# Casting loads in long runs, sliced attention, one-pass rsqrt and a moved g_norm in a linear-attention and bilinear-FFN kernel

## The chip, the cores and the metric

The kernel runs on one core of one Trainium2 chip. The metric is device time in microseconds (us), lower is better. Where several runs of a kernel exist, the median is given with the lowest and highest. Here a run counts as slow when it is over 1.5% above the fastest of the same kernel. One run of the kernel before (455.86 us, in the third group of rounds below) was slow; it is counted in the median of that group and left out of the ratios. The engines are called PE (TensorE), PEld (TensorE's weight loads), DVE (VectorE), ACT (ScalarE), POOL (GpSimd) and SP (SyncE), as the profile calls them.

## The reference, cut to what matters

```python
# q, k, v: (8 batches, 8 heads, 576, 64) fp32; g_norm: (64,)
kv  = np.einsum('bhsd,bhse->bhde', k, v)
out = np.einsum('bhsd,bhde->bhse', q, kv)
rms = np.sqrt(np.mean(out * out, axis=-1, keepdims=True) + 1e-06)
x   = (out / rms * g_norm)            # then (b, s, h*d): 4608 tokens x 512
a, b = x @ w_a, x @ w_b               # 512 x 1536 each
y   = (a * b) @ w_out                 # 1536 x 512, fp32 out
```

Linear attention per batch gives x. Two up projections are multiplied, and a down projection follows. In both kernels the matmuls run in bf16.

## The kernel before

q, k and v are loaded as fp32 by SyncE's queue, three loads per pair of heads and tensor. The two heads alternate in the tile, so that each run in it is one row of 64 values, 256 B. The matmuls read the upper halves of the fp32 words as bf16 (`bfview`). The weights go through GpSimd's queue, which casts them to bf16.

```python
def load_one(b, p, name, src):
    t = qkv_pool.tile([128, NCH + 1, 2, D], FP32, name=name, tag=name)
    for hl in range(2):
        nc.sync.dma_start(out=t[:, 0:NCH, hl, :],
            in_=src[b, 2 * p + hl, 0:SA, :].rearrange("(sp quar) d -> sp quar d", quar=NCH))
    nc.sync.dma_start(out=t[0:SB, NCH, :, :], ...)
```

Attention of a batch is a generator with three parts. The FFN units are another, and six units run after each part. A unit is one of 12 pairs of a/b products, or one of 4 output blocks, of a strip of 512 tokens. The last part of attention normalizes x. It takes 1/rms as Exp(-0.5 Ln(.)), four times per batch:

```python
for p in range(4):
    lns = asb_pool.tile([128, S], FP32, name="lns", tag="lns")
    nc.scalar.activation(lns[:, 0:SA], ssbA[p], AF.Ln, bias=eps_t, scale=1.0 / D)
    nc.scalar.activation(lns[:, SA:S], ssbB_sh[:, p, :], AF.Ln, bias=eps_t, scale=1.0 / D)
    sbc = asb_pool.tile([128, S], BF16, name="sbc", tag="sbc")
    nc.scalar.activation(sbc, lns, AF.Exp, scale=-0.5)
    nc.vector.tensor_mul(xt[p][:, tok0 : tok0 + S], xt[p][:, tok0 : tok0 + S], sbc)
yield
...
for b in range(B):                       # the schedule
    if b + 2 < B:
        loaded[b + 2] = load_b(b + 2)
    gen = attn_b(b, loaded.pop(b))
    for _ in gen:
        pump_ffn(6)
    ...                                  # strips whose tokens are done join the FFN queue
```

g_norm is multiplied into kv (a masked 128x128 VectorE multiply per pair of heads), and the ones matrix of the mean of squares is scaled by 1/g² to take it out again there.

Of the kernel before, what the change touches and what calls it, by code (L numbers as in the profile page):

```python
# [11 lines left out]


def bfview(t):
    u = t.bitcast(BF16)
    idx = tuple([slice(None)] * (len(u.shape) - 1) + [slice(1, None, 2)])
    return u[idx]
# [3 lines left out]
def kernel(  # L22
# [19 lines left out]
    SA = 512  # L42
    SB = S - SA
    NCH = S // 128
    STRIP = 512
    N_STRIP = n_tok // STRIP
    EPS = 1e-6

# [3 lines left out]
    qkv_pool = ctx.enter_context(tc.tile_pool(name="qkv", bufs=8))  # L52
    qst_pool = ctx.enter_context(tc.tile_pool(name="qst", bufs=12, space=bass.MemoryType.DRAM))
    asb_pool = ctx.enter_context(tc.tile_pool(name="asb", bufs=5))
    ab_pool = ctx.enter_context(tc.tile_pool(name="ab", bufs=2 * FC))
    osb_pool = ctx.enter_context(tc.tile_pool(name="osb", bufs=4))

    apsum = ctx.enter_context(tc.tile_pool(name="apsum", bufs=5, space=bass.MemoryType.PSUM))
    fpsum = ctx.enter_context(tc.tile_pool(name="fpsum", bufs=3, space=bass.MemoryType.PSUM))

    ident = const.tile([128, 128], BF16)
    make_identity(nc, ident)

    gmask = const.tile([128, 128], FP32)
    nc.vector.memset(gmask, 0.0)
    nc.gpsimd.dma_start(out=gmask[0:64, 0:64], in_=g_norm.partition_broadcast(64))
    nc.gpsimd.dma_start(out=gmask[64:128, 64:128], in_=g_norm.partition_broadcast(64))

    g_col = const.tile([128, 1], FP32)
    g_src = g_norm.rearrange("(d u) -> d u", u=1)  # L70
    nc.gpsimd.dma_start(out=g_col[0:64, :], in_=g_src)
    nc.gpsimd.dma_start(out=g_col[64:128, :], in_=g_src)
    invg2 = const.tile([128, 1], FP32)
    nc.vector.tensor_mul(invg2, g_col, g_col)
    nc.vector.reciprocal(invg2, invg2)
    bigmask = const.tile([128, 128], BF16)
    nc.vector.memset(bigmask, 0.0)
    nc.vector.memset(bigmask[0:64, 0:64], 1.0)
    nc.vector.memset(bigmask[64:128, 64:128], 1.0)
    nc.vector.tensor_scalar_mul(bigmask, in0=bigmask, scalar1=invg2)  # L80

    eps_t = const.tile([128, 1], FP32)
    nc.vector.memset(eps_t, EPS)

    wa_t = wpool.tile([128, KC, d_ff], BF16, name="wa_t")
    wb_t = wpool.tile([128, KC, d_ff], BF16, name="wb_t")
    wo_t = wpool.tile([128, FC, d_model], BF16, name="wo_t")

    def load_weights_ab():
        for kc in range(KC):  # L90
            nc.gpsimd.dma_start(
                out=wa_t[:, kc, :], in_=moe_w_a[kc * 128 : (kc + 1) * 128, :]
            )
            nc.gpsimd.dma_start(
                out=wb_t[:, kc, :], in_=moe_w_b[kc * 128 : (kc + 1) * 128, :]
            )

    def load_weights_o():
        for fc in range(FC):
            nc.gpsimd.dma_start(  # L100
                out=wo_t[:, fc, :], in_=moe_w_out[fc * 128 : (fc + 1) * 128, :]
            )

    xt = []
    for kc in range(KC):
        xt_t = xt_pool.tile([128, n_tok], BF16, name=f"xt{kc}", tag=f"xt{kc}")
        xt.append(xt_t)

    def load_one(b, p, name, src):
        t = qkv_pool.tile([128, NCH + 1, 2, D], FP32, name=name, tag=name)  # L110
        for hl in range(2):
            nc.sync.dma_start(  # L112
                out=t[:, 0:NCH, hl, :],
                in_=src[b, 2 * p + hl, 0:SA, :].rearrange(
                    "(sp quar) d -> sp quar d", quar=NCH
                ),
            )
        nc.sync.dma_start(  # L118
            out=t[0:SB, NCH, :, :],
            in_=src[b, 2 * p : 2 * p + 2, SA:S, :].rearrange("h sp d -> sp h d"),  # L120
        )
        return t

    def load_b(b):
        tiles = [{} for _ in range(4)]
        for p in range(4):
            tiles[p]["kt"] = load_one(b, p, "kt", k)
            tiles[p]["vt"] = load_one(b, p, "vt", v)
        for p in range(4):
            tiles[p]["qt"] = load_one(b, p, "qt", q)  # L130
        return tiles

    def attn_b(b, loaded):
        tok0 = b * S

        kv_sh = apsum.tile([128, 4, 128], FP32, name="kv_sh", tag="at")
        qT_ps = []
        for p in range(4):
            kt, vt = loaded[p]["kt"], loaded[p]["vt"]
            for c in range(NCH):  # L140
                nc.tensor.matmul(  # L141
                    kv_sh[:, p, :],
                    lhsT=bfview(kt[:, c, :, :]),
                    rhs=bfview(vt[:, c, :, :]),
                    start=(c == 0),
                    stop=False,
                )
            nc.tensor.matmul(  # L148
                kv_sh[:, p, :],
                lhsT=bfview(kt[0:SB, NCH, :, :]),  # L150
                rhs=bfview(vt[0:SB, NCH, :, :]),
                start=False,
                stop=True,
            )
        for p in range(4):
            qt = loaded[p]["qt"]
            qT = apsum.tile([128, S], BF16, name="qT_ps", tag="at")
            for c in range(NCH):
                nc.tensor.transpose(  # L159
                    qT[:, c * 128 : (c + 1) * 128], bfview(qt[:, c, :, :]), ident  # L160
                )
            nc.tensor.transpose(  # L162
                qT[:, SA:S], bfview(qt[0:SB, NCH, :, :]), ident[0:SB, 0:SB]
            )
            qT_ps.append(qT)
        kvg = []
        qT_sb = []
        for p in range(4):
            kvg_p = asb_pool.tile([128, 128], BF16, name="kvg", tag="kvg")
            nc.vector.tensor_mul(kvg_p, kv_sh[:, p, :], gmask)  # L170
            kvg.append(kvg_p)
            qs = asb_pool.tile([128, S], BF16, name="qT_sb", tag="qT_sb")
            nc.scalar.copy(qs, qT_ps[p])  # L173
            qT_sb.append(qs)
        yield

        xuA = []
        xuB_sh = apsum.tile([128, 4, SB], FP32, name="xuB_sh", tag="at")
        for p in range(4):
            xa = apsum.tile([128, SA], FP32, name="xuA", tag="at")  # L180
            nc.tensor.matmul(xa, lhsT=kvg[p], rhs=qT_sb[p][:, 0:SA], start=True, stop=True)  # L181
            nc.tensor.matmul(  # L182
                xuB_sh[:, p, :], lhsT=kvg[p], rhs=qT_sb[p][:, SA:S], start=True, stop=True
            )
            xuA.append(xa)
        sq_sb = []
        sqB_sh = asb_pool.tile([128, 4, SB], BF16, name="sqB_sh", tag="sqB_sh")
        nc.scalar.activation(sqB_sh, xuB_sh, AF.Square)
        for p in range(4):
            sq = asb_pool.tile([128, SA], BF16, name="sq_sb", tag="sq_sb")  # L190
            nc.scalar.activation(sq, xuA[p], AF.Square)  # L191
            sq_sb.append(sq)
            nc.vector.tensor_copy(xt[p][:, tok0 : tok0 + SA], xuA[p])
            nc.vector.tensor_copy(xt[p][:, tok0 + SA : tok0 + S], xuB_sh[:, p, :])
        yield

        ssbA = []
        ssbB_sh = apsum.tile([128, 4, SB], FP32, name="ssbB_sh", tag="at")
        nc.tensor.matmul(
            ssbB_sh.rearrange("a b c -> a (b c)"),  # L200
            lhsT=bigmask,
            rhs=sqB_sh.rearrange("a b c -> a (b c)"),
            start=True,
            stop=True,
        )
        for p in range(4):
            sa = apsum.tile([128, SA], FP32, name="ssbA", tag="at")
            nc.tensor.matmul(sa, lhsT=bigmask, rhs=sq_sb[p], start=True, stop=True)
            ssbA.append(sa)
        for p in range(4):  # L210
            lns = asb_pool.tile([128, S], FP32, name="lns", tag="lns")
            nc.scalar.activation(lns[:, 0:SA], ssbA[p], AF.Ln, bias=eps_t, scale=1.0 / D)  # L212
            nc.scalar.activation(  # L213
                lns[:, SA:S], ssbB_sh[:, p, :], AF.Ln, bias=eps_t, scale=1.0 / D
            )
            sbc = asb_pool.tile([128, S], BF16, name="sbc", tag="sbc")
            nc.scalar.activation(sbc, lns, AF.Exp, scale=-0.5)  # L217
            nc.vector.tensor_mul(  # L218
                xt[p][:, tok0 : tok0 + S], xt[p][:, tok0 : tok0 + S], sbc
            )  # L220
        yield

    def ffn_strip(s):
        t0 = s * STRIP
        ab_tiles = []
        for fc in range(FC):
# [68 lines left out]
    def pump_ffn(n):  # L295
        nonlocal cur_ffn
        for _ in range(n):
            while True:
                if cur_ffn is None:
                    if not ffn_q:  # L300
                        return
# [51 lines left out]
```

## Time and profile before

| | before |
|---|---|
| time, median of 3 runs | 450.46 us (450.39 to 453.36) |
| span of the profiled run | 446.9 us |
| PE busy | 349.9 us, 78% |
| ACT busy | 232.6 us, 52%, of which 65 table loads of 1.283 us: 83 us |
| steady TensorE work begins | about 70 us |

The page of the kernel before. The first line is each engine's busy time. The rows are 40 equal slices of the span (tenths for PE and PEclk, the granted TensorE clock). Then come the queues (packets, MB, share of 16 engines), the chain of waits by engine, and two groups (count, busy us, mean ns, idle before).

```profile
PE 349.9 (78%) x1720; PEld 160.6 (36%) x1720; DVE 142.6 (32%) x280; ACT 232.6 (52%) x341; POOL 13.6 (3%) x30
...
PE   0002548997699869987998699879986994999995
...
PEclk9999999999599979999999799989999999999999
...
GB/s 132 208 199 151 154 145 145 145 19 49 152 137 150 97 137 150 135 121 167 138 150 103 155 151 60 12 84 0 2 23 70 1 0 29 67 0 80 16 1 94
...
q1 hardware_dynamic: 115200, 28.33, 28.6%
...
PE 47%; ACT 31%; SPq 10%; issue 3%; DMA 3%; DVE 3%; ACTq 2%; DVEq 0%
...
L217 ACT ACT_TABLE_LOAD x32 | 41.1, 1283 | 0.6
L213 ACT ACT_TABLE_LOAD x30 | 38.5, 1283 | 0.5
```

Two losses stand in it. The PE row is empty for three slices and at most half full for the next three. After that it dips about once per batch, and the clock dips with it. ScalarE carries 31% of the chain.

The timeline of the kernel before, in three stretches (start us, duration us, engine, line, operation, output<-input, count, and in brackets the idle time before it and its releaser). SPq is SyncE's issuing; L213 and L217 are Ln and Exp:

```profile
45.07 1.28 SPq L112 DMA_DIRECT2D qt<-in_q_dram  x2
...
141.64 1.28 ACT L213 ACT_TABLE_LOAD   x1
142.94 0.31 ACT L213 ACTIVATE lns<-ssbB_sh,eps_t 128x64 f32<-128x64 f32 x1
143.15 1.26 ACT L212 ACTIVATE lns<-ssbA,eps_t 128x512 f32<-128x512 f32 x2
144.43 1.28 ACT L217 ACT_TABLE_LOAD   x1
145.72 0.68 ACT L217 ACTIVATE sbc<-lns 128x576 bf16<-128x576 f32 x1
...
159.57 0.59 PE L233 MATMUL a_ps<-xt_109,wa_t 128*128 128x512 bf16 x1 [1.34 <-DVE o_sb L263]
159.95 0.63 PE L233 MATMUL a_ps<-xt_110,wa_t 128*128 128x512 bf16 x1
...
162.87 0.38 PE L233 MATMUL a_ps<-xt_109,wa_t 128*128 128x512 bf16 x1
...
166.46 0.59 PE L241 MATMUL b_ps<-xt_109,wb_t 128*128 128x512 bf16 x1 [2.56 <-ACT a_sb L249]
```

SyncE issues a load every 0.63 us, and that alone sets the pace from 35 us on: the GB/s row is flat near 150 to about 90 us. From 141.6 to 158.4 us ScalarE does nothing but Ln, Exp and the loads between them, beside issuing two stores, and each pair of passes pays two loads.

The windows view of the kernel before shows what that costs TensorE. The first column is the stretch and the next its length, then busy us of PE, PEld, DVE, ACT and POOL with counts, then the granted clock, the DMA share and GB/s:

```profile
0.00:70.30 70.30, 16.39 (x72) 7.44 (x73) 6.97 (x24) 22.74 (x30) 13.59 (x30) 1.00 0.82 164
70.30:446.90 376.60, 333.54 (x1648) 153.19 (x1647) 135.62 (x256) 209.87 (x311) 0.00 (x0) 0.96 0.35 83
...
166.00:170.00 4.00, 3.54 (x10) 1.31 (x10) 1.38 (x2) 0.97 (x3) 0.00 (x0) 0.57 0.73 165
141.00:158.00 17.00, 15.86 (x97) 7.92 (x94) 2.67 (x5) 16.72 (x21) 0.00 (x0) 1.00 0.48 108
158.00:166.00 8.00, 4.56 (x15) 1.74 (x14) 3.05 (x8) 2.77 (x6) 0.00 (x0) 0.79 0.61 145
```

While ScalarE switches tables (141 to 158 us) TensorE still has queued units and is busy 15.9 of 17 us. The loss comes after it. From 158 to 170 us it is busy 8.1 of 12 us, and at a granted clock of 0.79 and then 0.57. The chain of waits there runs through what had piled up behind the passes on ScalarE: the issuing of stores, the landing of one (2.31 us) and four copies of q (2.25 us). After TensorE's wait at 159.57 us the matmuls run about 0.43 us apart up to 162.87 us, and then 0.216 us apart; after the wait at 166.46 us the same happens again. The Trainium skill, "TensorE: Matmul & The Clock Gate", Part 1, calls this a clock gate: the array starts at half rate and reaches the full one after about 3.4 us of sustained work. The trace agrees on that length (3.3 us).

### The profile page before, as it was taken

The page shows a single profiled execution, that of the slowest core. Times are in us where ns is not written, and L with a number is a line of the kernel's source. Part 1 is how long each engine was busy: PE and PEld are TensorE (multiplying, and loading weights), DVE is VectorE, ACT ScalarE, POOL GpSimd, SP SyncE. Part 2 cuts the span into 40 slices and gives each one's busy share as a digit, 9 for nine tenths or more (in the row PEclk, how much of TensorE's full clock was granted, in tenths as well). Part 3 has the DMA queues.
Part 4 walks back from the last instruction along what each step waited for, and adds up shares of the span by engine and source line. Part 5 has one row for each costly group of instructions (what it writes and reads, how often), then busy time and mean ns, then how long its engine had stood idle before and what let it go on. Part 6 is the DMA issues. An engine that isn't in the chain of part 4 may idle for free.

```text
span 446.9 us, 4884 instructions
## 1 busy us (share of the span) xinstructions
PE 349.9 (78%) x1720; PEld 160.6 (36%) x1720; DVE 142.6 (32%) x280; ACT 232.6 (52%) x341; POOL 13.6 (3%) x30
## 2 busy tenths in 40 slices
PE   0002548997699869987998699879986994999995
PEld 0001213443244424443444244434443441444442
DVE  0000212351353134414621353146214623332431
ACT  1000694589255944595579346945793587330320
POOL 6220000000000000000000000000000000000000
PEclk9999999999599979999999799989999999999999
DMA  6996666601566456556664662030002001202004
GB/s 132 208 199 151 154 145 145 145 19 49 152 137 150 97 137 150 135 121 167 138 150 103 155 151 60 12 84 0 2 23 70 1 0 29 67 0 80 16 1 94
DMA packets 123736, 42.83 MB, mean 96 GB/s; under 512 B 116512, under 2 KB 118080, under 8 KB 123712
## 3 DMA queue, kind: packets, MB, share of 16 engines
q1 hardware_dynamic: 115200, 28.33, 28.6%
q10 hardware_dynamic: 5504, 9.44, 7.9%
q0 software_dynamic: 3008, 4.75, 5.8%
q8 instruction: 13, 0.21, 0.2%
q14 instruction: 11, 0.09, 0.1%
HBM read 37.78 MB, written 9.44 MB: 106 GB/s over the span
## 4 chain that ended last, share of the span: by engine, by line
PE 47%; ACT 31%; SPq 10%; issue 3%; DMA 3%; DVE 3%; ACTq 2%; DVEq 0%
PE b_ps L241 20%; PE a_ps L233 20%; ACT L213 9%; ACT L217 8%; SPq L112 6%; ACT sbc L217 5%; PE o_ps L255 5%; SPq L118 4%; ACT lns L212 3%; ACT qT_sb L173 3%; ACTq L275 2%; ACT lns L213 2%; DVE o_sb L263 2%; PE xuA L181 2%; DMA out_dram<-o_sb 2%
## 5 line engine op out<-in xcount | busy, mean ns | idle before, releaser
L249 ACT CAST a_sb<-a_ps 128x512 bf16<-128x512 f32 x108 | 63.3, 593 | 113.7 <-PE a_ps L233 96.8
L241 PEld LDWEIGHTS <-wb_t 128*128 128x128 bf16 x432 | 43.7, 101 | 77.5 <-issue 31.8
L233 PEld LDWEIGHTS <-wa_t 128*128 128x128 bf16 x432 | 42.8, 101 | 66.0 <-issue 22.8
L173 ACT COPY qT_sb<-qT_ps 128x576 bf16<-128x576 bf16 x32 | 19.0, 647 | 77.6 <-PE qT_ps L162 53.3
L233 PE MATMUL a_ps<-xt_109,wa_t 128*128 128x512 bf16 x108 | 43.5, 403 | 14.9 <-DVE o_sb L263 14.0
L241 PE MATMUL b_ps<-xt_109,wb_t 128*128 128x512 bf16 x108 | 43.1, 400 | 13.0 <-ACT a_sb L249 12.9
L233 PE MATMUL a_ps<-xt_110,wa_t 128*128 128x512 bf16 x108 | 43.4, 402 | 3.1 <-DVE xt_110 L218 3.1
L233 PE MATMUL a_ps<-xt_111,wa_t 128*128 128x512 bf16 x108 | 43.2, 400 | 2.3 <-DVE xt_111 L218 2.3
L233 PE MATMUL a_ps<-xt_112,wa_t 128*128 128x512 bf16 x108 | 42.8, 397 | 1.9 <-DVE xt_112 L218 1.9
L141 PE MATMUL kv_sh<-vt,kt 128*128 128x128 bf16 x128 | 14.0, 236 | 37.5 <-DMA vt<-in_v_dram 37.5
L241 PE MATMUL b_ps<-xt_110,wb_t 128*128 128x512 bf16 x108 | 43.2, 400 | 0.0
L241 PE MATMUL b_ps<-xt_111,wb_t 128*128 128x512 bf16 x108 | 43.1, 399 | 0.0
L241 PE MATMUL b_ps<-xt_112,wb_t 128*128 128x512 bf16 x108 | 42.8, 397 | 0.0
L217 ACT ACT_TABLE_LOAD x32 | 41.1, 1283 | 0.6
L213 ACT ACT_TABLE_LOAD x30 | 38.5, 1283 | 0.5
L263 DVE COPY o_sb<-o_ps 128x512 f32<-128x512 f32 x36 | 23.5, 685 | 15.0 <-PE o_ps L255 15.0
L141 PEld LDWEIGHTS <-kt 128*128 128x128 bf16 x128 | 9.1, 104 | 42.8 <-issue 39.7
L217 ACT ACTIVATE sbc<-lns 128x576 bf16<-128x576 f32 x32 | 21.9, 683 | 0.4
L212 ACT ACTIVATE lns<-ssbA,eps_t 128x512 f32<-128x512 f32 x32 | 20.9, 682 | 0.0
L191 ACT ACTIVATE sq_sb<-xuA 128x512 bf16<-128x512 f32 x32 | 17.8, 610 | 5.0 <-PE xuB_sh L182 3.0
L159 PE MATMUL qT_ps<-ident,qt 128*128 128x128 bf16 x128 | 13.9, 237 | 5.0 <-DMA qt<-in_q_dram 5.0
L170 DVE TENSOR_TENSOR kvg<-kv_sh,gmask 128x128 bf16<-128x128 f32 x32 | 7.0, 281 | 33.6 <-PE kv_sh L148 33.6
(374 smaller groups left out, 423.9 us busy)
## 6 DMA issues: line engine op xcount, KB each, us to landing
kt<-in_k_dram SPq DMA_DIRECT2D x64, 128.0 KB, 2.9
vt<-in_v_dram SPq DMA_DIRECT2D x64, 128.0 KB, 2.8
qt<-in_q_dram SPq DMA_DIRECT2D x64, 128.0 KB, 2.8
out_dram<-o_sb ACTq DMA_DIRECT2D x40, 128.0 KB, 2.4
out_dram<-o_sb ACTq DMA_DIRECT2D x16, 256.0 KB, 2.5
wa_t<-in_moe_w_a_dram POOLq DMA_DIRECT2D x4, 384.0 KB, 11.2
wb_t<-in_moe_w_b_dram POOLq DMA_DIRECT2D x4, 384.0 KB, 12.8
wo_t<-in_moe_w_out_dram POOLq DMA_DIRECT2D x12, 128.0 KB, 8.3
```

Of the source, the lines that this page charges most:

```text
L112: nc.sync.dma_start(out=t[:, 0:NCH, hl, :], in_=src[b, 2 * p + hl, 0:SA, :].rearrange("(sp quar) d -> sp quar d", quar=NCH),)
L118: nc.sync.dma_start(out=t[0:SB, NCH, :, :], in_=src[b, 2 * p : 2 * p + 2, SA:S, :].rearrange("h sp d -> sp h d"),)
L141: nc.tensor.matmul(kv_sh[:, p, :], lhsT=bfview(kt[:, c, :, :]), rhs=bfview(vt[:, c, :, :]), start=(c == 0), stop=False,)
L173: nc.scalar.copy(qs, qT_ps[p])
L212: nc.scalar.activation(lns[:, 0:SA], ssbA[p], AF.Ln, bias=eps_t, scale=1.0 / D)
L213: nc.scalar.activation(lns[:, SA:S], ssbB_sh[:, p, :], AF.Ln, bias=eps_t, scale=1.0 / D)
L217: nc.scalar.activation(sbc, lns, AF.Exp, scale=-0.5)
L233: nc.tensor.matmul(a_ps, lhsT=wa_t[:, kc, fc * 128 : (fc + 1) * 128], rhs=xt[kc][:, t0 : t0 + STRIP], start=(kc == 0), stop=(kc == KC - 1),)
L241: nc.tensor.matmul(b_ps, lhsT=wb_t[:, kc, fc * 128 : (fc + 1) * 128], rhs=xt[kc][:, t0 : t0 + STRIP], start=(kc == 0), stop=(kc == KC - 1),)
L249: nc.scalar.copy(a_sb, a_ps)
L255: nc.tensor.matmul(o_ps, lhsT=ab_tiles[fc][:, g * 128 : (g + 1) * 128], rhs=wo_t[:, fc, :], start=(fc == 0), stop=(fc == FC - 1),)
L263: nc.vector.tensor_copy(o_sb, o_ps)
```

## The change

It has four intents, in one rewrite. (A slice is a piece of a batch's attention; "hoisted" below means that the build put an operation into an engine's queue ahead of work that does not need it.)

1. q, k and v come through GpSimd's casting queue, a half or a whole tensor of a batch per load, in runs of 1 KB read and 512 B written. VectorE then reorders k and q with copies.
2. Attention is cut into slices (kv of a pair, transposes of a pair, x of 288 columns), and one slice stands after every FFN unit.
3. Ln and Exp become one `Abs_reciprocal_sqrt`.
4. g_norm is applied at x, in the VectorE operation that also multiplies by 1/rms.

The rewrite also moves some work between engines: q's transposed copy goes to VectorE, kv's copy and half of the output copies to ScalarE, the stores to SyncE's queue. Weight loads get other shapes, and the buffers for TensorE's results are split in another way.

The core of the diff. Names of pools, the store's helper and the FFN loops, whose arithmetic is the same, are cut:

```diff
-    def load_one(b, p, name, src):
-        t = qkv_pool.tile([128, NCH + 1, 2, D], FP32, name=name, tag=name)
-        for hl in range(2):
-            nc.sync.dma_start(out=t[:, 0:NCH, hl, :], ...)
+    def load_b(b, parts):
+        for name in ("k", "v", "q"):
+            tiles[name] = qkv_pool.tile([128, H, NCH + 1, D], BF16, name=name + "t", tag=name)
+            if name != "v":
+                tiles[name + "r"] = qkv_pool.tile(
+                    [128, NCH + 1, H, D], BF16, name=name + "r", tag=name + "r", bufs=2)
+        ...
+                nc.gpsimd.dma_start(out=t[:, hs, 0:NCH, :],
+                    in_=src[b, hs, 0:SA, :].rearrange("h (sp c) d -> sp h c d", c=NCH))
+                nc.gpsimd.dma_start(out=t[0:SB, hs, NCH, :],
+                    in_=src[b, hs, SA:S, :].rearrange("h sp d -> sp h d"))
...
+    def reorder(t, name, hs):
+        nc.vector.tensor_copy(t[name + "r"][:, 0:NCH, hs, :],
+            t[name][:, hs, 0:NCH, :].rearrange("p h c d -> p c h d"))
+        nc.vector.tensor_copy(t[name + "r"][0:SB, NCH, hs, :], t[name][0:SB, hs, NCH, :])
...
-            nc.vector.tensor_mul(kvg_p, kv_sh[:, p, :], gmask)
+            nc.scalar.copy(self.kvd[0:D, p, 0:D], self.kv_ps[0:D, p, 0:D])
+            nc.scalar.copy(self.kvd[D:, p, D:], self.kv_ps[D:, p, D:])
...
-            nc.scalar.activation(lns[:, 0:SA], ssbA[p], AF.Ln, bias=eps_t, scale=1.0 / D)
-            nc.scalar.activation(lns[:, SA:S], ssbB_sh[:, p, :], AF.Ln, bias=eps_t, scale=1.0 / D)
-            nc.scalar.activation(sbc, lns, AF.Exp, scale=-0.5)
-            nc.vector.tensor_mul(xt[p][...], xt[p][...], sbc)
+            nc.scalar.activation(rs, ps, AF.Abs_reciprocal_sqrt, bias=eps_t)
+            nc.vector.scalar_tensor_tensor(out=xt[p][:, t0 : t0 + HF],
+                in0=self.x_ps[p, h], scalar=g_col, in1=rs, op0=ALU.mult, op1=ALU.mult)
...
-        for _ in gen:
-            pump_ffn(6)
+    loaded[0] = load_b(0, 2)              # then w_a and w_b
+    loaded[1] = load_b(1, 2)              # then w_out
+    loaded[2] = load_b(2, 1)
+    drain(Attn(0, loaded.pop(0), 2).slices())
+    for fc in range(FC):
+        ffn_ab(0, fc)
+    drain(Attn(1, loaded.pop(1), 2).slices())
+    for s in range(1, N_STRIP):
+        ...                               # load_b(s + 2, 1); gen = Attn(s + 1, ...).slices()
+        for fc in range(FC):
+            ffn_ab(s, fc)
+            step(gen)
+            if fc % 3 == 2:
+                ffn_o(s - 1, fc // 3)
+                step(gen)
+        if gen is not None:
+            drain(gen)
```

## The prediction

> **What bounds the kernel now.** TensorE is busy 78% (page, part 1). In plain FFN stretches a 128x512 matmul starts every 0.216 us (timeline: 48 output matmuls in 10.36 us); 1296 of them are 280 us of the 446.9 us span. Attention needs about 6 us of TensorE per batch (timeline: 0.46 us per five transposes or kv matmuls), 47 us in all. The other 120 us are waiting:
> 1. Start. The first FFN matmul runs at 58 us, steady flow begins near 70 us. Until 35 us the DMA engines are full (share 0.9 to 1.2, windows), weights mixed with q/k/v; after that SyncE issues one load per 0.63 us (timeline), 150 GB/s.
> 2. Per batch, Ln/Exp: 64 table loads of 1.28 us (82 us of ScalarE, groups). The chain of waits runs through them for about 14 us in every batch; after such waits TensorE's first eight matmuls start 0.43 us apart (timeline).
>
> **What the change does.** One reciprocal-square-root pass replaces Ln and Exp; one table load is left in the built program. Per half-sequence (288 columns) I estimate, taking 0.83 ns per column off the 512-wide times, a Square of 0.42 us, an rsqrt of 0.50 and a VectorE multiply of 0.5. ScalarE falls from 233 to about 150 us; VectorE rises from 143 to about 180 (reorder copies and transposed q added). Both stay under TensorE. Attention slices stand between FFN units in the built order, so their ScalarE work hides under 1.73 us units: the 14 us stalls should go. TensorE work stays about the same.
>
> **What it adds.** All loads go through one casting queue in order. 256 B packets (115200, 17.8 ns each by part 3) become 1 KB reads cast to 512 B writes; the Trainium skill, "DMA: Bandwidth & Descriptors", Specifications, gives 512 B as the line-rate minimum, and this trace's casting queue read 364 GB/s while its packets ran (9.44 MB in 5.8% of 16 engines). I estimate 300 GB/s.
> But the built VectorE order puts the reorder copies of batches 2 and 3 inside attention of batch 1, and VectorE is in order. So strip 1 cannot start before q of batch 3 has landed: 23.6 MB, 79 us at 300 GB/s, plus 3: 82 us. By then TensorE has done only attention 0 and 1 and strip 0's a/b. This gives back most of the better start.
>
> **Sum.** 82 us, then eight strips of a/b (166), nine of output (93), six attentions (34), last copy and store (4): 379. Small waits 4, time over span 3.5 (450.46 against 446.9): 386 us.
>
> Range 364 to 412: at 370 GB/s the start takes 67 us, at 230 GB/s 106.
> Faster by over 2%: 97%; within 2%: 2%; slower: 1%.
>
> **What would show it.**
> - Groups: ACT_TABLE_LOAD x1; ScalarE near 150 us; no FFN matmuls waiting on xt after the start.
> - Timeline of VectorE at 45 to 90 us: reorder copies waiting for k and q DMAs, TensorE idle with them; strip 1 steady near 82 us.
> - After that TensorE over 95% busy, no 0.43 us restarts.
> - Casting queue about 300 GB/s up to 80 us.
>
> **What would make it wrong.** Casting of 512 B rows, or descriptor generation for 512 rows per load, slower than seen here (0.54 us per load of 128 rows). The skill, "SBUF — State Buffer", Who interferes with whom, says VectorE copies in two-port mode block GpSimd's descriptors; the reorder copies could do that (this trace has no such copy, so does not show it). ScalarE queueing in the rsqrt slices (1.5 us per 2.0 us unit) stalling TensorE. Or a faster queue: then 365.

## The result

| | before | after |
|---|---|---|
| time, median | 451.08 us (450.39 to 453.36, 4 runs) | 370.08 us (369.17 to 371.11, 4 runs) |
| ratio of the fast runs, 95% interval | 1 | 0.8216 (0.8179 to 0.8253) |
| PE busy | 349.9 us, 78% | 341.7 us, 93% |
| ACT busy | 232.6 us | 140.2 us |

The four runs of before here are the three above and one made later. The ratios are from the fast runs of both kernels in the same rounds, so they are not quite the ratios of the medians.

The page of the kernel after, the lines that answer to those of before:

```profile
PE 341.7 (93%) x1744; PEld 163.8 (44%) x1744; DVE 149.7 (41%) x268; ACT 140.2 (38%) x320; POOL 57.6 (16%) x80
...
PE   0588859999999999999999999999999999999994
...
PEclk9999885699999999999999999999999999999998
...
GB/s 96 177 196 192 165 193 192 191 191 204 210 32 30 69 51 31 29 73 49 28 30 28 28 30 29 30 28 29 30 28 30 28 28 30 29 28 59 28 58 85
...
q0 software_dynamic: 45728, 18.88, 41.5%
...
PE 81%; DMA 11%; POOL 3%; ACT 2%; DVE 1%; issue 1%; POOLq 0%; ACTq 0%; DVEq 0%
...
L188 ACT ACTIVATE sq<-x_ps 128x288 bf16<-128x288 f32 x64 | 26.1, 411 | 33.2 <-PE x_ps L180 32.8
L196 ACT ACTIVATE rs<-s_ps,eps_t 128x288 f32<-128x288 f32 x64 | 31.7, 498 | 1.9 <-PE s_ps L194 1.7
```

One table load is left in the whole program. ScalarE fell from 31% to 2% of the chain. The GB/s row stands near 190, counted in bytes written, from about 10 to 80 us (177 to 196, with one dip to 165). The casting queue writes bf16 and reads fp32, so 192 is 384 GB/s read.

The windows view of the kernel after, at the point from which its TensorE flow is steady:

```profile
50.00:60.00 10.00, 5.77 (x33) 3.11 (x32) 3.77 (x7) 1.41 (x5) 3.97 (x6) 0.66 1.57 192
60.00:70.00 10.00, 8.95 (x37) 3.93 (x36) 5.49 (x13) 6.32 (x17) 5.41 (x7) 0.50 1.58 192
...
0.00:72.30 72.30, 49.70 (x223) 23.16 (x223) 28.96 (x66) 25.42 (x62) 44.10 (x64) 0.86 1.38 175
72.30:369.40 297.10, 292.00 (x1522) 140.64 (x1521) 120.78 (x203) 114.79 (x258) 13.48 (x16) 1.00 0.30 54
```

From 72.3 us on TensorE is busy 98% at full clock, and the work that was left takes 297.1 us. The steady flow starts as late as in before (72.3 against 70.3 us), but by then 49.7 instead of 16.4 us of TensorE work is done (223 instead of 72 matmuls). In the first 20 us TensorE is busy 6.8 us, while the first loads come in. The rest of the start's loss lies mostly between 50 and 70 us: waits, and a clock of 0.66 and 0.50.

The timeline of the kernel after in that stretch (L126 is the reorder copy):

```profile
53.30 0.69 DVE L126 COPY kr<-kt 128x2048 bf16<-128x2048 bf16 x1 [6.21 <-DMA kt<-in_k_dram]
...
54.84 0.59 PE L233 MATMUL b_ps<-xt_122,wb_t 128*128 128x512 bf16 x1 [4.23 <-DVE abt L243]
55.22 0.63 PE L233 MATMUL b_ps<-xt_123,wb_t 128*128 128x512 bf16 x1
...
69.27 0.88 POOL L86 DMA_DIRECT2D kt<-in_k_dram  x1 [1.51 <-DMA qt<-in_q_dram]
69.54 1.10 DVE L126 COPY qr<-qt 128x2048 bf16<-128x2048 bf16 x1
```

At 53.3 us VectorE had waited 6.2 us for k of batch 2, to make a copy that attention 2 needs only later. The build had put this copy into VectorE's queue ahead of the multiplies of strip 0's last units, and they ran only after it, so TensorE waited 4.2 us too, and restarted 0.43 us apart. The last hoisted copy, q of batch 3, started at 69.54 us; its load's landing was first seen at about 69.3 us. Strip 1 becomes steady right after it.

### The profile page after: what moved, and what is told of

It reads as the page before. It is cut to its first block, busy times and chain, and to the rows that moved or that the text cites. A ratio compares the mean times of both kernels' runs of the same rounds, so it can differ in the third digit from the quotient of the medians.

```text
span 369.4 us, 4627 instructions
## 1 busy us (share of the span) xinstructions
PE 341.7 (93%) x1744; PEld 163.8 (44%) x1744; DVE 149.7 (41%) x268; ACT 140.2 (38%) x320; POOL 57.6 (16%) x80
## 3 DMA queue, kind: packets, MB, share of 16 engines
q0 software_dynamic: 45728, 18.88, 41.5%
q1 hardware_dynamic: 5664, 9.44, 9.2%
HBM read 37.75 MB, written 9.44 MB: 128 GB/s over the span
## 4 chain that ended last, share of the span: by engine, by line
PE 81%; DMA 11%; POOL 3%; ACT 2%; DVE 1%; issue 1%; POOLq 0%; ACTq 0%; DVEq 0%
PE o_ps L269 26%; PE a_ps L233 23%; PE b_ps L233 22%; DMA kt<-in_k_dram 4%; PE kv_ps L154 3%; PE q_ps L171 3%; DMA wa_t<-in_moe_w_a_dram 3%; DMA qt<-in_q_dram 2%; PE s_ps L194 2%; DMA vt<-in_v_dram 2%; PE x_ps L180 2%; POOL wb_t L67 1%; POOL wa_t L66 1%; ACT rs L196 1%; ACT sq L188 0%
## 5 line engine op out<-in xcount | busy, mean ns | idle before, releaser
L243 DVE TENSOR_TENSOR abt<-b_ps,a_sb 128x512 bf16<-128x512 f32 x108 | 74.4, 691 | 100.7 <-PE b_ps L233 94.2
L269 PE MATMUL o_ps<-wo_t,abt 128*128 128x512 bf16 x432 | 98.6, 379 | 0.0
L269 PEld LDWEIGHTS <-abt 128*128 128x128 bf16 x432 | 41.3, 98 | 46.7
L188 ACT ACTIVATE sq<-x_ps 128x288 bf16<-128x288 f32 x64 | 26.1, 411 | 33.2 <-PE x_ps L180 32.8
L196 ACT ACTIVATE rs<-s_ps,eps_t 128x288 f32<-128x288 f32 x64 | 31.7, 498 | 1.9 <-PE s_ps L194 1.7
L154 PE MATMUL kv_ps<-vt,kr 128*128 128x128 bf16 (+1 forms) x160 | 20.2, 241 | 13.0 <-DMA vt<-in_v_dram 12.0
L280 DVE COPY o_sb<-o_ps 128x512 f32<-128x512 f32 x18 | 12.5, 692 | 38.3 <-PE o_ps L269 38.3
L278 ACT COPY o_sb<-o_ps 128x512 f32<-128x512 f32 x18 | 10.5, 586 | 45.4 <-PE o_ps L269 45.4
L154 PEld LDWEIGHTS <-kr 128*128 128x128 bf16 (+1 forms) x160 | 13.9, 105 | 24.4 <-issue 6.9
L194 PE MATMUL s_ps<-sq,ones 128*128 128x288 bf16 x64 | 19.7, 308 | 1.8 <-ACT rs L196 0.7
```

Source lines behind the costliest of these rows:

```text
L154: nc.tensor.matmul(self.kv_ps[:, p, :], lhsT=kt[0:r, c, hs, :], rhs=vt[0:r, hs, c, :], start=(c == 0), stop=(c == NCH),)
L188: nc.scalar.activation(sq, ps, AF.Square)
L194: nc.tensor.matmul(ps, lhsT=ones, rhs=self.sq[p, h], start=True, stop=True)
L196: nc.scalar.activation(rs, ps, AF.Abs_reciprocal_sqrt, bias=eps_t)
L243: nc.vector.tensor_mul(t, b_ps, a_sb)
L269: nc.tensor.matmul(o_ps, lhsT=ab[s, fc][:, g * 128 : (g + 1) * 128], rhs=wo_t[:, fc, :], start=(fc == 0), stop=(fc == FC - 1),)
```

## The experiments

There were twelve runs. All gave correct results. Each was timed in 3 or 5 rounds beside the kernel before, whose medians in the three groups of rounds were 450.98, 451.35 and 450.56 us.

| kernel | median (range), us | ratio to before (95% interval) |
|---|---|---|
| before, one-pass rsqrt alone | 385.10 (384.93 to 385.98) | 0.8538 (0.8467 to 0.8610) |
| before, casting loads alone | 416.29 (414.90 to 420.48) | 0.9238 (0.9141 to 0.9335) |
| before, both | 368.28 (367.27 to 368.98) | 0.8171 (0.8135 to 0.8206) |
| after, Ln and Exp | 511.02 (507.36 to 511.22) | 1.1297 (1.1194 to 1.1399) |
| after, attention unsliced | 394.10 (392.87 to 395.55) | 0.8742 (0.8666 to 0.8819) |
| after, g_norm into kv | 370.49 (369.37 to 372.16) | 0.8229 (0.8194 to 0.8264) |
| after, short runs, no copies | 374.90 (374.05 to 376.64) | 0.8312 (0.8264 to 0.8360) |
| after, one copy buffer | 365.71 (364.42 to 366.04) | 0.8099 (0.8063 to 0.8136) |
| after, attention 1 among strip 0 | 364.52 (363.96 to 365.37) | 0.8079 (0.8043 to 0.8115) |
| after, these two | 363.72 (363.27 to 365.54) | 0.8070 (0.8028 to 0.8111) |
| after, w_out loaded later | 368.58 (367.66 to 370.06) | 0.8184 (0.8150 to 0.8218) |
| after, all three | 359.13 (358.38 to 361.05) | 0.7979 (0.7945 to 0.8013) |

The theory at the outset had two parts. First, the table loads were the loss in every batch, so removing them gains most. Second, the hoisted copies tie the start to later loads. The rival to the first was that the fine slices do the hiding, or the better loads. The rival to the second was that the queue's rate alone sets the start, so a changed order would not help.

### Which part of the change carries the time

**One-pass rsqrt alone, in the kernel before.**

```diff
-            nc.scalar.activation(lns[:, 0:SA], ssbA[p], AF.Ln, bias=eps_t, scale=1.0 / D)
-            nc.scalar.activation(lns[:, SA:S], ssbB_sh[:, p, :], AF.Ln, bias=eps_t, scale=1.0 / D)
-            nc.scalar.activation(sbc, lns, AF.Exp, scale=-0.5)
+            nc.scalar.activation(sbc[:, 0:SA], ssbA[p], AF.Abs_reciprocal_sqrt, bias=eps_t, scale=1.0 / D)
+            nc.scalar.activation(sbc[:, SA:S], ssbB_sh[:, p, :], AF.Abs_reciprocal_sqrt, bias=eps_t, scale=1.0 / D)
```

> The kernel before with only Ln and Exp replaced by one Abs_reciprocal_sqrt pass (loads, order and slices as before). Theory: the table loads in the Ln/Exp chain are what stops TensorE in every batch, so this part alone brings most of the gain: the chain loses about 10.3 us of table loads and 2.4 us of Ln per batch; 385 to 400 us, with 2 table loads left. Rival (the gain needs the slices or the new loads; a wait of the same size takes the place of the table loads): 420 us or more.

It measured 385.1 us: 66 us less, from this edit alone, and at the lower end of what was expected. Two table loads are left. The chain of waits by engine on its page, and one of its windows:

```profile
PE 85%; SPq 11%; issue 1%; ACT 1%; DMA 1%; DVE 0%
```

```profile
120.00:160.00 40.00, 39.79 (x209) 19.11 (x212) 18.30 (x36) 17.49 (x37) 0.00 (x0) 1.00 0.69 164
```

ScalarE all but left the chain (1%), and TensorE is busy 39.8 of every 40 us between 80 and 320 us. This is with the old, coarse schedule: the slices are not needed to hide the work that is left. The start stays slow, with SyncE's issuing (SPq) at 11% of the chain.

**Casting loads alone, in the kernel before.** The loader and `reorder` of after, with the matmuls reading their tiles and fewer, larger buffers for them; nothing else changed:

```diff
-            kt, vt = loaded[p]["kt"], loaded[p]["vt"]
+            kt, vt = loaded["kr"], loaded["v"]
+            if p % (4 // parts) == 0:
+                reorder(loaded, "k", slice(2 * p, 2 * p + 8 // parts))
...
-    loaded[0] = load_b(0)
+    loaded[0] = load_b(0, 2)
```

> The kernel before with only the loads changed: all through the casting queue in long runs, and the reorder copies on VectorE. Theory: only the start gets shorter, since from about 70 us on loads were ahead anyway; 430 to 445 us, with the 14 us Ln/Exp stalls unchanged. Rival (loads bind in every batch): 400 us or less.

It measured 416.3 us, a gain of 35 us, more than was expected and less than the rival said. In the windows view TensorE has been busy 52.2 us by 80 us, against 26.1 us in before. That accounts for about 26 us. The two profiled runs differ by 31.6 us, less than the medians; of the other 5.5 us, 3.4 are TensorE's idle time after 80 us (39.6 instead of 43.0 us), and the cause of the rest was not traced. The table loads are all still there, and TensorE is busy only 33.5 to 37 of each 40 us from 80 to 280 us.

**Ln and Exp back, in the kernel after.** The first activation at the program's start becomes Ln too.

```diff
-            nc.scalar.activation(rs, ps, AF.Abs_reciprocal_sqrt, bias=eps_t)
+            ln = asb_pool.tile([128, HF], FP32, name="ln", tag="ln")
+            nc.scalar.activation(ln, ps, AF.Ln, bias=eps_t)
+            nc.scalar.activation(rs, ln, AF.Exp, scale=-0.5)
```

> The kernel after with Ln and Exp put back in each half-sequence slice (128 table loads in the built program, 164 us). Theory: the slices only hide ScalarE work if it is short; with 3.1 us more per slice ScalarE needs about 4.6 us per slice against about 2 us of TensorE, so TensorE waits in all 64 slices: 480 to 520 us, slower than the kernel before. Rival (slices hide it, ScalarE total of about 336 us being under TensorE's): 370 to 390 us.

It measured 511.0 us, slower than before. The timeline of ScalarE in it:

```profile
139.87 0.41 ACT L188 ACTIVATE sq<-x_ps 128x288 bf16<-128x288 f32 x1
140.30 1.28 ACT L197 ACT_TABLE_LOAD   x1
141.59 0.50 ACT L197 ACTIVATE ln<-s_ps,eps_t 128x288 f32<-128x288 f32 x1
142.11 1.28 ACT L198 ACT_TABLE_LOAD   x1
143.40 0.44 ACT L198 ACTIVATE rs<-ln 128x288 f32<-128x288 f32 x1
...
144.22 0.41 ACT L188 ACTIVATE sq<-x_ps 128x288 bf16<-128x288 f32 x1
```

A slice takes 4.35 us of ScalarE from one Square to the next, while an FFN unit takes 1.73 us of TensorE. The fine slices double the number of table loads (127 in the groups, beside the first one), and they put each of them between two units. ScalarE hardly waits here (busy 19.7 of 20 us from 130 to 150 us); it is the bottleneck of these stretches. With the table loads still there, fine slices cost time: before with the casting loads runs the same passes in coarse steps in 416.3 us.

**Both edits in the kernel before, without slices and with g_norm where it was.** The edit is the sum of the first two.

> The kernel before with both other parts: one rsqrt pass and the casting loads with their reorder copies, but its own coarse order (attention in three steps, six FFN units after each). Apart these parts gave 66 us (385.1) and 35 us (416.3). Theory: the per-batch stall is gone with the table loads already, so the fine half-sequence slices add nothing over the coarse steps, and what is left is the start: 362 to 374 us, within 2% of the kernel after. Rival (the slices are worth a part of their own): 378 us or more.

It measured 368.3 us, ratio 0.8171, against 0.8216 for the whole change: the intervals overlap. So the fine slices add nothing to rsqrt and loads with the old coarse steps, nor, on balance, does anything else in the rewrite. After the start the windows view also rules out a gain that something else cancels: from 90 us on TensorE is full in both, busy 269.96 of 270 us here (to 360 us) and 272.79 of 273 us in after (to 363 us), at a clock of 1.00. The gains of the two edits do not add: 66 and 35 us alone, 82 us together. Its VectorE too waits for k and q of later batches (the last time at 81.3 us, for q of batch 4).

**Attention not sliced, in the kernel after.** Each batch's attention is drained after the strip.

```diff
         for fc in range(FC):
             ffn_ab(s, fc)
-            step(gen)
             if fc % 3 == 2:
                 ffn_o(s - 1, fc // 3)
-                step(gen)
         if gen is not None:
             drain(gen)
```

> The kernel after with the attention of batch s+1 issued in one piece after the FFN of strip s instead of in slices among its units. Theory: the chain from x over Square, sum and rsqrt takes some 10 to 12 us per batch of which TensorE works 6, so 5 to 7 us per batch for six batches: 395 to 415 us. Rival (the slices add nothing, one pass of rsqrt is short enough): within 2% of the kernel after, 370 to 377 us.

It measured 394.1 us, 24 us more than after and 1 us under the expected range. In its chain of waits Square and rsqrt pieces of 0.4 to 0.5 us stand between TensorE's pieces at every batch, and from 72 us to its end it takes 319 us where after takes 297. Some interleaving is needed; what before had is enough.

**g_norm into kv, in the kernel after.** VectorE scales kv by a table of g (here called `gmask`), the ones matrix is scaled by 1/g² (cut here), and x takes a plain multiply.

```diff
-            nc.scalar.copy(self.kvd[0:D, p, 0:D], self.kv_ps[0:D, p, 0:D])
-            nc.scalar.copy(self.kvd[D:, p, D:], self.kv_ps[D:, p, D:])
+            nc.vector.tensor_mul(self.kvd[0:D, p, 0:D], self.kv_ps[0:D, p, 0:D], gmask[0:D, :])
+            nc.vector.tensor_mul(self.kvd[D:, p, D:], self.kv_ps[D:, p, D:], gmask[D:, :])
...
-            nc.vector.scalar_tensor_tensor(out=xt[p][...], in0=self.x_ps[p, h], scalar=g_col, in1=rs, ...)
+            nc.vector.tensor_mul(xt[p][:, t0 : t0 + HF], self.x_ps[p, h], rs)
```

> The kernel after with g_norm taken back from x into kv (two 64x64 VectorE multiplies per pair by a g table instead of ScalarE copies, the ones matrix scaled by 1/g squared, a plain multiply by rsqrt at x). Theory: the place of g_norm carries no time, since VectorE and ScalarE are far from full: within 1% of the kernel after, 367 to 374 us. Rival (it shortens a chain): 378 us or more.

It measured 370.5 us, against 370.1, and the intervals overlap. Where g_norm is applied carries no time that these runs can show.

### What the start costs, and why

**Short runs without reorder copies, in the kernel after.** k and q are loaded straight into the order that the matmuls read, one load per quarter: 256 B reads and 128 B writes. These tiles get three buffers.

```diff
+                if name != "v":
+                    sv = src[b, hs, 0:SA, :].rearrange("h (sp c) d -> sp c h d", c=NCH)
+                    for c in range(NCH):
+                        nc.gpsimd.dma_start(out=r[:, c, hs, :], in_=sv[:, c, :, :])
...
-            self.need("k", p)
...
-            self.need("q", p)
```

> The kernel after with k and q loaded straight into the reordered layout (256 B reads, 128 B writes, four times as many packets for them), v and weights still in long runs, no reorder copies on VectorE. Theory: long runs are what makes one queue fast enough: the start loses 10 to 25 us to the queue although the copies are gone: 380 to 395 us. Rival (the packets cost the same by byte, and the copies were the only loss): 360 to 366 us.

It measured 374.9 us, between the two expectations and 5 us worse than after, although the copies and their waits are gone. From its page (busy times, then the casting queue):

```profile
PE 337.2 (91%) x1710; PEld 162.4 (44%) x1744; DVE 133.8 (36%) x228; ACT 140.0 (38%) x320; POOL 105.2 (28%) x140
...
q0 software_dynamic: 95840, 18.88, 61.1%
```

The same 18.88 MB took 61.1% of the engines' time instead of 41.5%, and GpSimd, which issues these loads, was busy 105 instead of 58 us. The long runs are worth more than the copies cost, but not by much as long as the copies also hold up VectorE. The run does not separate the length of the runs from the number of loads: from 10 to 20 us GpSimd issued without a pause while only 101 GB/s were written.

**One buffer for the reordered tiles.** With a single buffer, a batch's copies cannot be made before the attention of the batch before it has read its own; this was meant to take those of batches 2 and 3 out of the start.

```diff
-                    [128, NCH + 1, H, D], BF16, name=name + "r", tag=name + "r", bufs=2
+                    [128, NCH + 1, H, D], BF16, name=name + "r", tag=name + "r", bufs=1
```

> The kernel after with one buffer instead of two for the reordered k and q, so that the reorder copies of batches 2 and 3 can no longer stand ahead of the work of attention 1 in VectorE's queue. Theory: the start is held by those copies waiting for their loads (6.2 us for k of batch 2 at 47 to 53 us, and 1.1 us of a copy at 69.5 us, with TensorE's restart at half rate after it); without them strip 1 starts 6 to 10 us earlier: 360 to 364 us. Rival (attention 1 is held by its own chain and by loads): 368 us or more.

It measured 365.7 us: 4 us gained, less than expected. The timeline shows why. VectorE now waits for q of batch 2, still inside attention 1:

```profile
58.50 0.69 DVE L126 COPY qr<-qt 128x2048 bf16<-128x2048 bf16 x1 [3.47 <-DMA qt<-in_q_dram]
```

**Attention 1 among strip 0's units.** Its own chain, which ran serially from 57 to 72 us, is stepped twice after each of strip 0's last eight units.

```diff
+    gen = Attn(1, loaded.pop(1), 2).slices()
     for fc in range(FC):
         ffn_ab(0, fc)
-    drain(Attn(1, loaded.pop(1), 2).slices())
+        if fc >= 4:
+            for _ in range(2):
+                step(gen)
+    drain(gen)
```

> The kernel after with attention 1 stepped twice per unit from the fifth FFN unit of strip 0 on, instead of after it, two buffers for the reordered k and q. Theory: the reorder copies of later batches still stand in VectorE's queue and now hold up strip 0 as well, so little is gained: 362 to 372 us. Rival (the serial attention 1 is what costs, not the queue of VectorE): 350 to 358 us.

It measured 364.5 us, inside the range of its theory: VectorE still waited 4.75 us for k of batch 2, and TensorE 3.3 us behind it. **Both of these edits:**

> Both edits: attention 1 among the FFN units of strip 0, and one buffer for the reordered k and q. Theory: strip 1 starts at about 50 to 55 us instead of 72: 350 to 356 us. If the loads of batch 1 (landed at about 41 us) hold TensorE up in strip 0, 356 to 362 us.

It measured 363.7 us, which is outside what either theory expected, and not to be told from one of the edits (0.8070 against 0.8079, intervals overlapping). The wait had moved again, to k of batch 2. The timeline of the kernel with both edits:

```profile
52.70 0.69 DVE L126 COPY kr<-kt 128x2048 bf16<-128x2048 bf16 x1 [7.19 <-DMA kt<-in_k_dram]
...
55.03 0.40 PE L180 MATMUL x_ps<-qs,kvd 128*128 128x288 bf16 x1 [5.74 <-DVE xt L198]
```

TensorE was idle for 5.7 us behind it. So k of batch 2 had to come earlier. In the load order w_out stood ahead of it (1.57 MB in bf16, 3.15 MB read, 8 us at 384 GB/s), and w_out is first used in strip 1.

**w_out behind batch 2's loads.**

```diff
-    for i in range(2):
-        load_o(i, FC // 2)
     loaded[2] = load_b(2, 1)
+    for i in range(2):
+        load_o(i, FC // 2)
```

> The kernel after with the loads of w_out put behind those of batch 2 instead of ahead of them; nothing else changes. Theory: in the start, VectorE waits for k of batch 2 (landed at 53.2 us behind 3.1 MB of w_out); with k of batch 2 ahead it lands some 8 us earlier and strip 1 starts 5 to 8 us earlier: 362 to 366 us. Rival (q of batch 3, whose place in the queue is the same, sets the start): 368 us or more.

Alone it measured 368.6 us, 1.5 us less than after, which is within the noise (the intervals overlap), and a miss. The number lies where the rival (the landing of q of batch 3) had put it, but the trace shows another wait. k of batch 2 was now copied at 44.45 us instead of 53.30, but with two copy buffers the next hoisted copy, k of batch 3, took the wait over, and TensorE waited 4.5 us behind it. For q of batch 3 VectorE then waited only 0.25 us. Its timeline:

```profile
61.52 0.69 DVE L126 COPY kr<-kt 128x2048 bf16<-128x2048 bf16 x1 [4.84 <-DMA kt<-in_k_dram]
```

**All three edits.**

> Three edits together: attention 1 among the FFN units of strip 0, one buffer for the reordered k and q, and w_out behind batch 2. In the run with only the first two, VectorE still waited for k of batch 2 until 52.2 us and TensorE restarted at half rate. Theory: with that load earlier, strip 1 starts near 50 us instead of 60: 353 to 358 us. If w_out, now last, arrives too late for the first output unit: 358 to 362 us.

It measured 359.1 us, 1 us above the range, and faster than both kernels. It lies where a late w_out had been expected to put it, but w_out was not late: its loads took at most 15.6 us from issue to landing, the last was issued at 42.3 us, and the first output matmul at 63.7 us shows no wait. What is left is a copy again: VectorE waited 3.64 us for q of batch 2, until 49.92 us. In its timeline one TensorE wait of more than 1 us is left between 40 and 75 us, and its window from 60 us on is full at full clock:

```profile
51.89 0.28 PE L180 MATMUL x_ps<-qs,kvd 128*128 128x288 bf16 x1 [2.88 <-DVE xt L198]
```

```profile
60.00:70.00 10.00, 10.00 (x59) 4.99 (x58) 4.19 (x7) 3.05 (x8) 4.69 (x6) 1.00 1.58 192
```

The three edits gain 4.4, 5.6 and 1.5 us alone (medians against 370.1), and 11 us together. The first two together gain only 6.4 us; the third adds 4.6 us to them (medians of different rounds; about 4 us by the ratios). The rate hardly differed: from 10 to 70 us 187 GB/s were written in after and 189 to 193 in these five runs. So at least these 11 us of after's start were held by the order in which VectorE and the queue were given their work, and not by the rate.

## Why the prediction was right or wrong

It predicted 386 us, range 364 to 412, and faster by over 2% at 97%. 370.1 us lies in the range, 16 us under the centre.

- **"Per batch, Ln/Exp": right about the cause.** Removing Ln and Exp alone took 66 us off, and putting them back into after cost 141 us. The step "the 14 us stalls should go" mixed two things. 14 to 17 us is the length of ScalarE's chain, and most of it lay under queued TensorE work (15.9 of 17 us busy in the window shown). TensorE's loss per batch was about 8 us. Before needs 376.6 us from 70.3 us on, and with rsqrt alone the same remaining work takes about 321 us from 62 us on: 56 us over the seven batches whose passes come after that point. Of these, 37 us are idle time (43.1 against 6.1 us). The sum did not use the 14, so nothing came of it.
- **"Attention slices stand between FFN units ... so their ScalarE work hides": not what did it.** It hides, but it hides as well in the old coarse steps. Rsqrt and loads without slices gave 0.8171 against 0.8216. Only taking all interleaving away costs (24 us). The sum did not depend on it.
- **"The built VectorE order puts the reorder copies of batches 2 and 3 inside attention of batch 1": right.** The copies are seen there, waiting. The three edits that took them and attention 1's serial chain away gained 11 us. The start came out where the rule "landing of q of batch 3, plus 3 us" puts it (69.3 and 72.3 us). Whether the landing of q of batch 3 itself held after, as the prediction put it, stays open. It landed at about 69.3 us, just when VectorE came to it, and the wait that TensorE shows is the earlier one for k of batch 2, with attention 1's own chain at half clock after it.
- **"I estimate 300 GB/s": the mis-sized term.** The queue read 384 GB/s at its steady rate. From 1.25 us to the landing at 69.3 us it averaged 23.6 MB (9.44 of weights and four batches of 3.54) / 68.0 us = 347 GB/s, mainly because the first 10 us run at about half of 384. The start took 72.3 us and not 82. That is 9.7 of the 16 us.
- **"Small waits 4, time over span 3.5".** The work after the start took 297.1 us against 166 + 93 + 34 + 4 = 297, so the 4 us of waits did not show. That is in part luck: about ten matmuls of strip 1 and five of attention 2, some 3 us, ran before 72.3 us, and TensorE was not busy in 5.1 of the 297.1 us. Time over span was 1.7 us (371.11 against 369.4). The estimate of 3.5 had compared a median with the span of what seems to have been another run. These two give 3.9 and 1.8 us. With 9.7 they make 15.4 us, from the unrounded 386.5 to the profiled run's 371.1.
- **Durations of the slices: right.** Square 0.42 estimated, 0.411 measured; rsqrt 0.50 and 0.498; the VectorE multiply 0.50 and 0.518. ScalarE came out at 140 us (150 estimated), VectorE at 150 (180 estimated); neither bounds anything.
- **"No 0.43 us restarts" after the start: right**, with a clock of 1.00 from 72.3 us on.
- **VectorE copies and GpSimd descriptors, named as a risk: some copies and issues ran longer while they overlapped, and others did not** (last section).

## What to carry to other kernels

When a pair of ScalarE functions switches tables inside a per-batch chain, replace the pair before rearranging anything. That one edit gave 66 us, while slicing with the pair still there cost more than it hid. A copy for a later batch, put into an engine's queue ahead of present work, ties that work to the later batch's load. Look at the built order and at what each copy waits for, and expect that removing one such wait uncovers the next: here the third edit gave 1.5 us alone and 4.6 us on top of the other two. With a casting queue, say whether its rate counts bytes read or written (here 384 or 192 GB/s). Take the length of a chain on one engine for a loss only where the bottleneck engine is really idle.

## What the Trainium skill lacked or had wrong

- "ScalarE: Activation LUTs", What ACT_TABLE_LOAD costs, gives about 1283 ns for the load, which all traces here show, and about 1380 ns of drain on top, 2.66 us per switch. These traces show no such drain time: in the kernel after with Ln and Exp back, the load starts 0.02 us after the pass before it and the next pass 0.01 us after the load, so a switch cost 1.31 us.
- The same page, Table sets, says that ln followed by exp takes one load, because one set has both. The program built here loaded at every change between them: 64 loads for Ln and Exp in before, and 127 in the run with the slices. The page should say that a build may not choose the common set; the count of loads in the profile's groups shows it. It does not mention `Abs_reciprocal_sqrt`, which was correct in every run here that used it, in one pass of 498 ns for 288 columns.
- "DMA: Bandwidth & Descriptors", Specifications, lists about 358 GB/s as the HBM limit per core. The casting queue here read 384 GB/s from 50 to 70 us. That is no contradiction once Measured is read too: there the page has 425 GB/s at 16 MB on one core, and says that about 358 is each core's part when both cores of a pair stream. This kernel ran on one core; the table should say so. The page has no rate for a queue that casts, and doesn't say whether bytes read or written are then to be counted (192 GB/s written here). Which of the two is the limit no run here shows.
- The same page, Anatomy of one DMA, which is about loads that GpSimd issues, calls the time of descriptor generation "small, variable". On GpSimd the main load of k or q of a whole batch cost 0.88 us of issue, and the 80 loads of k's and q's quarters took 0.87 and 0.88 us each on average in the run with short runs. For SyncE's queue, which that table doesn't cover, 0.63 us per load set a ceiling near 150 GB/s in before.
- "SBUF — State Buffer", Who interferes with whom, says that a VectorE copy in a two-port mode and GpSimd's descriptor writing shut each other out. In the traces some overlaps took longer, in both directions, by 0.3 to 0.4 us. The copy of q at 69.54 us, begun while GpSimd was issuing, took 1.10 instead of 0.69 us. The issue below took 1.20 instead of 0.88 us while copies ran, and the second copy 0.65 instead of 0.28 us. But the copy of q at 59.46 us (0.69 us) and the issue at 59.90 us (0.88 us) overlapped and were no longer than usual. No experiment isolated it, and no trace shows the copies' mode. The timeline of the kernel after:

```profile
86.35 1.20 POOL L86 DMA_DIRECT2D vt<-in_v_dram  x1 [5.88 <-PE kv_ps L154]
...
86.98 0.65 DVE L130 COPY kr<-kt 64x512 bf16<-64x512 bf16 x1
```

- "TensorE: Matmul & The Clock Gate", Part 1, says that the clock falls back to half after an idle window of about 3.4 us, and tells of a kernel whose clock swung because of frequent short waits. In before it was at half rate after waits of 1.34 and 2.56 us (the timeline at 159.57 and 166.46 us). In the start of after the half rate lasted from 54.8 to about 70 us, with TensorE busy 8.95 of 10 us in the second half of it and single waits of 0.35 us or less between matmuls there. The page does not say how much waiting inside a window brings the clock down or keeps it there; these runs show only that it is less than a whole idle window.
